# A block-sorted attention followed by a gated feed-forward layer: an earlier issue for the first weights, another place in the queue for batch 1's values, and rows of 72 elements for the mixed values

## The chip, the cores and the metric

The kernel runs on one core of one Trainium2 chip. The metric is the device time of one execution in microseconds (us); lower is better. Five engines work beside each other and meet through semaphores: PE (TensorE, matrix products; PEld in the profile is its loading of the stationary operand), DVE (VectorE), ACT (ScalarE), POOL (GpSimd) and SP (SyncE). Transfers between device memory and on-chip SBUF run on 16 DMA engines. PSUM holds the results of matrix products until DVE or ACT moves them to SBUF.

## The reference

```python
# B, H, S, D = 4, 8, 768, 64; 8 blocks of 96 rows; d_model 512, d_ff 1536
P = sort_net                                   # (B, H, 8, 8)
for _ in range(5):                             # Sinkhorn: rows, then columns
    P = exp(P - max(P, -1)); P = P / sum(P, -1); P = P / sum(P, -2)
k_sorted = einsum('bhij,bhjcd->bhicd', P, k_blocks)   # mix whole blocks
v_sorted = einsum('bhij,bhjcd->bhicd', P, v_blocks)
scores = q_blocks @ k_sorted.T / sqrt(D)       # inside a block: 96 x 96
attn = softmax(scores); o = attn @ v_sorted    # (B, H, S, D)
x = o as (B*S, H*D)                            # 3072 tokens of 512
g = x @ w_gate; out = (silu(g) * (x @ w_val)) @ w_out
```

## The kernel before

**Stages.** All loads are cast to bf16 on the way. The Sinkhorn iterations run first, on DVE and ACT, while batch 0's values, queries and keys arrive. The mixing weights P become a block matrix (`rmix`), and PE mixes the blocks of values (`v_chunk`, L275), keys (`k0_chunk`, L264, for batch 0; `kq_chunk`, L244, for the others) with it. Batch 0's attention for the first half of the tokens is written out by hand. From there on the feed-forward layer runs in eight steps `ffn(0)` to `ffn(7)`, one for each half batch of 384 tokens: 12 column blocks, each a gate product (`gate`, L385) and a value product (`value`, L403) of four matmuls, and with each step the output products of the step before (`outp`, L420). ACT takes the tanh of a gate product (L393), DVE makes gate times sigmoid of it (`gs_sb`, L395), and DVE multiplies the value product by that (`h`, L408).

**The order on PE.** PE and POOL run in the order in which the program writes them. `merge` places side work among the feed-forward products: a side item carries a due time, and it goes out once the running cost of the products written (0.65 for a gate or value product, 0.87 for a third of an output product) has reached it. These due times are numbers in the code, not measurements. In `ffn(1)` the side work is the mixing of batch 1: four `v_chunk` of 16 of the 64 value columns each, then three `kqs` items of two `kq_chunk` each, then the attention of batch 1 (`units`). DVE and ACT are ordered by a scheduler in that stage.

**PSUM.** Gate, value and early output products share three buffers (tag "gen"), so a product waits until DVE has read the product three before it. The mixes use two wide buffers, "a" and "b", in turn; each is drained by DVE or ACT (`drain`, L222 and L224).

**Loads.** POOL issues all loads, in one queue, and in between it copies values into a layout with the 96 rows of a block innermost (`copy_v`, L124, from `v_tiles` to `vch`); a `v_chunk` reads `vch` and needs all copies of its columns. Each POOL copy of 64 x 1536 elements is one quarter of the rows of a block. The order at the start: batch 0's values in two halves, the first query load, batch 0's keys in two halves, three copies, the first weights, the second query load, more weights with batch 1's values among them, batch 1's keys and queries, the output weights. The weights of `w_gate` and `w_val` come in six pairs of 256 columns each, which is two column blocks of the feed-forward layer:

```python
    def load_gv(lo, hi):
        load_w(wg_sb, wg_dram, lo, hi)
        load_w(wv_sb, wv_dram, lo, hi)
```

After these, POOL waits for batch 1's values, copies them (four copies), and issues the loads for batches 2 and 3.

**The mixed values.** `vt_tile` holds the mixed values, for each batch, head and block one row of 64 values, a one (its product gives the sum of the softmax), and padding. `av` (L334) multiplies the exponentials of a block (stationary, 96 x 128) by 65 elements of such a row; one call is eight matmuls over two heads and four blocks, in the order of the rows:

```python
                nc.tensor.matmul(o[:, two, i4, 0:D + 1], lhsT=e[:, i4 * C:i4 * C + 128],
                                 rhs=vt[:, 2 * g + two, half * 4 + i4, 0:D + 1],
```

There are 32 calls of `av`, four in the part written by hand and 28 among the feed-forward products.

Of the kernel before, what the change touches and what calls it, by code (L numbers as in the profile page):

```python
# [10 lines left out]
BF16 = mybir.dt.bfloat16  # L11
# [6 lines left out]
def kernel(  # L18
# [13 lines left out]
    B, H, S, D = q.shape  # L32
    NB = sort_net.shape[-1]
    C = S // NB
# [5 lines left out]
    DF = moe_w_gate.shape[1]  # L40
# [17 lines left out]
    vtp = ctx.enter_context(tc.tile_pool(name="vtp", bufs=2))  # L58
# [32 lines left out]
    def load_k(b, lo, hi):  # L91
        rows = highr if b else lowr
        nc.gpsimd.dma_start(out=kq_tile(b)[rows, lo:hi, :], in_=k_nat[b, :, lo:hi, :])
# [10 lines left out]
    def load_v(b, lo, hi):  # L104
        if b // 2 not in v_tiles:
            v_tiles[b // 2] = vnp.tile([128, C, D], BF16, name=f"v{b // 2}", tag="vn")
        u = b % 2
        nc.gpsimd.dma_start(out=v_tiles[b // 2][u * R:(u + 1) * R, lo:hi], in_=v_nat[b, :, lo:hi, :])

    def load_w(sb, dram, lo, hi):  # L110
        nc.gpsimd.dma_start(out=sb[:, :, lo:hi], in_=dram[:, :, lo:hi])
# [5 lines that stand above are left out]
    def copy_v(eng, pair, rows, s, n=4, d0=0, d1=D):  # L117
        cs = slice(s * (C // n), (s + 1) * (C // n))
        dst = vch3[rows, d0:d1, cs]
        src = v_tiles[pair][rows, cs, d0:d1]  # L120
        if eng is nc.scalar:
            eng.copy(dst, src.transpose([0, 2, 1]))  # L122
        else:
            eng.tensor_copy(dst, src.transpose([0, 2, 1]))  # L124
# [16 lines left out]
    def load_q0(t):  # L141
        nc.gpsimd.dma_start(out=q0[t].rearrange("p c d -> p (c d)"), in_=q_runs[0, t])
# [4 lines left out]
    load_q0(0)  # L147
    for a, rows in enumerate(halves):
        nc.gpsimd.dma_start(out=k0[rows], in_=k_nat[0, :, a * HC:(a + 1) * HC, :])
    copy_v(nc.gpsimd, 0, lowr, 0)  # L150
    copy_v(nc.gpsimd, 0, lowr, 3)
    copy_v(nc.gpsimd, 0, lowr, 5, 8, 40, D)
    load_gv(0, 256)
    load_q0(1)
    for m in range(256, 1024, 256):
        load_gv(m, m + 256)
    load_v(1, 0, C)
    for m in range(1024, DF, 256):
        load_gv(m, m + 256)
    load_k(1, 0, C)  # L160
    load_q(1, 0, C)
    nc.gpsimd.dma_start(out=wo_sb, in_=wo_dram)
# [6 lines left out]

    def vt_tile(pair):  # L170
        if pair not in vts:
            t = vtp.tile([C, 2, H * NB, D + 4], BF16, name=f"vt{pair}", tag="vt")
            nc.vector.memset(t[:, :, :, D:D + 1].rearrange("p u n e -> p (u n) e"), 1.0)
            vts[pair] = t
        return vts[pair]

    for pair in range(B // 2):
        vt_tile(pair)
# [59 lines left out]
    def kq_chunk(b, at, n, eng, tag):  # L238
        dst = kqt_tile(b)[:, 0:2 * GI * C].rearrange("p (n c) -> p n c", c=C)
        rm = rmix[b].rearrange("p a (g two) i -> p two (a g) i", two=2)  # L240
        tp = chunk_tile("tkq", n // 8, tag).rearrange("p (l n) -> p l n", n=2 * GI)
        for lc in range(n):
            for two in range(2):
                nc.tensor.matmul(tp[two * D:(two + 1) * D, lc, :],  # L244
                                 lhsT=kq_tiles[b][:, at + lc, :],
                                 rhs=rm[:, two], start=True, stop=True)
        drain(eng, dst[:, :, at:at + n], tp.transpose([0, 2, 1]))
# [20 lines left out]
    def v_chunk(b, at, n, eng, tag):  # L268
        rows = slice(0, 128) if b % 2 else lowr
        dst = vt_tile(b // 2)[:, b % 2]  # L270
        mix = rmix[b][rows, 0].rearrange("p a b -> p (a b)")
        tp = chunk_tile("tv", n // 8, tag).rearrange("p (l n) -> p l n", n=H * NB)
        for ld in range(n):
            col = (at + ld) * C
            nc.tensor.matmul(tp[:, ld, :], lhsT=vch[rows, col:col + 128], rhs=mix,  # L275
                             start=True, stop=True)
        drain(eng, dst[:, :, at:at + n], tp[0:C].transpose([0, 2, 1]))
# [103 lines left out]
    def gate(n, m):  # L381
        xt = xts[divmod(n, 2)]
        g_ps = psum.tile([128, TW], FP32, name="g_ps", tag="gen", bufs=3)
        for kc in range(NKC):
            nc.tensor.matmul(g_ps, lhsT=wg_sb[:, kc, ts(m, 128)], rhs=xt[:, kc, :],  # L385
                             start=(kc == 0), stop=(kc == NKC - 1))
        gate_out(n, m, g_ps)
# [11 lines left out]
    def value(n, m):  # L399
        xt = xts[divmod(n, 2)]  # L400
        v_ps = bank_tile("v_ps", "x" if (n, m) == (0, 1) else "gen")[:, 0:TW]
        for kc in range(NKC):
            nc.tensor.matmul(v_ps, lhsT=wv_sb[:, kc, ts(m, 128)], rhs=xt[:, kc, :],  # L403
                             start=(kc == 0), stop=(kc == NKC - 1))
        value_out(n, m, v_ps)
# [7 lines left out]
    def outp(n, t3, part):  # L413
        b, half = divmod(n, 2)
        h_w = h_tiles[n]
        if part == 0:
            o_tiles[n] = bank_tile("o_ps", "x" if 2 <= n < 2 * B - 1 or n == 2 * B - 1 and t3 == 1 else "gen")
        o_ps = o_tiles[n]
        for m in range(part * 4, part * 4 + 4):
            nc.tensor.matmul(o_ps, lhsT=h_w[:, m, ts(t3, 128)], rhs=wo_sb[:, m, :],  # L420
                             start=(m == 0), stop=(m == NFC - 1))
        if part < 2:
            return
        o_sb = opool.tile([128, DM], FP32, name="o_sb", tag="o_sb")
        nc.scalar.copy(o_sb, o_ps)  # L425
        base = b * S + half * TW + t3 * 128
        nc.sync.dma_start(out=out[ds(base, 128), :], in_=o_sb)
# [113 lines left out]
    def units(b, us, ats, lags=(3.1, 3.1)):  # L541
        us = list(us)
        todo = []
        for n, at in enumerate(ats):
            u, u2 = us[2 * n:2 * n + 2]
            lag = lags[n]
            held = []
            todo.append((at, lambda u=u, u2=u2, held=held: (qk(b, u, "b"), held.append(scores(b, u2, "a")))))
            todo.append((at + 1.3, lambda u2=u2, held=held: exps(b, u2, *held[0])))
            for w, tag, t in ((u, "b", 1.9), (u2, "a", 3.6)):  # L550
                if b == 0 or b == 1 and u < H2:
                    todo.append((at + t, lambda w=w, tag=tag: av(b, w, tag)))
                    todo.append((at + t + lag, lambda w=w: drain("v", *xtr(b, w))))
                else:
                    todo.append((at + t, lambda w=w, tag=tag: (av(b, w, tag), x_dma(b, w))))
        return todo

    def kqs(b, ats):
        return [(at, lambda n=n: (kq_chunk(b, n * 32, 16, "v", "b"), kq_chunk(b, n * 32 + 16, 16, "s", "a")))
                for n, at in enumerate(ats)]  # L560

    def vs(f, size, ats):
        return [(at, lambda m=m: f(1, m * size, size, "sv"[m % 2], "ba"[m % 2])) for m, at in enumerate(ats)]
# [5 lines left out]
    def merge(main, side):  # L569
        done, k = 0.0, 0  # L570
        side = sorted(side, key=lambda t: t[0])
        for c, f in main:
            f()
            done += c
            while k < len(side) and side[k][0] <= done:
                side[k][1]()
                k += 1
        while k < len(side):
            side[k][1]()
            k += 1  # L580

    def ffn(n):
        todo = []
        for m in range(NFC):
            if n > 0 or m > 1:
                todo.append((0.65, lambda m=m: gate(n, m)))
            if n > 0 or m > 0:
                todo.append((0.65, lambda m=m: value(n, m)))
            ends = (6, 9, 11) if n == 1 else (3, 7, 11)
            if n > 0 and m in ends:  # L590
                for part in range(3):
                    todo.append((0.87, lambda t3=ends.index(m), part=part: outp(n - 1, t3, part)))
        return todo
# [9 lines left out]
    def q0_rest():  # L603
# [1 line left out]
        q0_chunk(1, 16, 8, "v", "a")  # L605

    merge(ffn(0), [(0.0, q0_rest)] + units(0, range(4, 8), (2.0, 6.6)))
    merge(ffn(1), vs(v_chunk, 16, (3.2, 3.9, 4.7, 5.5)) + kqs(1, (6.2, 8.2, 10.3))
          + units(1, range(4), (11.3, 16.4), (3.1, 2.5)))
    for s in range(4):  # L610
        copy_v(nc.gpsimd, 1, both, s)
# [43 lines left out]
```

## Time and profile before

| | |
|---|---|
| time, median of 3 runs | 248.45 us (248.39 to 252.37) |
| profiled execution | 249.62 us |
| its span, first to last instruction | 247.7 us |
| TensorE clock granted | 1.000 |
| PE busy | 239.4 us, 97% |
| DVE, ACT, POOL busy | 157.1, 109.5, 51.9 us |
| loads through POOL's queue | 14.16 MB |

The profile is of one execution, and every time of a row is counted in us from the span's first instruction. The time of an execution contains the span and what lies around it, here 249.62 against 247.7. Matmuls overlap, so a busy time of PE that is close to the span says that PE hardly ever stops, not that each matmul is at its best. A row's idle time is that of its engine just before it; the name behind the arrow is the last event that was seen before the engine went on.

### The profile page before, as it was taken

How to read it: one execution, taken by the hardware profiler on the slowest of the kernel's cores; microseconds unless marked ns; L12 is line 12 of the kernel's file. 1: busy time of each engine (PE TensorE's matmuls, PEld its weight loads, DVE VectorE, ACT ScalarE, POOL GpSimd, SP SyncE). 2: the span in 40 equal slices, each digit the busy share in tenths (PEclk: the TensorE clock that was granted, in tenths of full speed). 3: DMA queues.
4: the chain of work that ended last, by engine and by line, in shares of the span. 5: the costliest groups of instructions: out<-in, count | busy, mean ns of one | idle time of the engine just before them, and what ended most of it. 6: DMA issues, size and time to landing. Idle time of an engine off the chain costs nothing.

```text
span 247.7 us, 6185 instructions
## 1 busy us (share of the span) xinstructions
PE 239.4 (97%) x2633; PEld 140.7 (57%) x2633; DVE 157.1 (63%) x332; ACT 109.5 (44%) x186; POOL 51.9 (21%) x45
## 2 busy tenths in 40 slices
PE   8799998999999999999999999999999999999995
PEld 6375665666555556655555655565555555555543
DVE  6686789787556775857657646755764585446700
ACT  3877652453544444444642552354245334232311
POOL 5993459960049300000000000000000000000000
PEclk9999999999999999999999999999999999999999
DMA  5999999999999287010122121112111121100122
GB/s 98 214 120 181 218 191 219 194 227 215 215 164 179 41 201 173 4 42 3 45 56 52 55 62 34 44 42 78 32 42 45 39 57 54 42 21 25 42 81 88
DMA packets 39578, 24.38 MB, mean 98 GB/s; under 512 B 27712, under 2 KB 35648, under 8 KB 39104
## 3 DMA queue, kind: packets, MB, share of 16 engines
q0 software_dynamic: 21376, 14.16, 39.3%
q1 hardware_dynamic: 18176, 9.84, 13.9%
q8 instruction: 20, 0.33, 0.5%
q14 instruction: 6, 0.05, 0.1%
HBM read 28.32 MB, written 7.86 MB: 146 GB/s over the span
## 4 chain that ended last, share of the span: by engine, by line
PE 83%; DVE 9%; ACT 2%; issue 2%; DMA 2%; DVEq 0%; POOLq 0%
PE v_ps L403 23%; PE o_ps L420 23%; PE g_ps L385 22%; PE tkq L244 3%; PE av_ps L334 2%; PE qk L307 2%; DVE st L340 2%; DMA v<-in_v_dram 2%; DVE gs_sb L395 2%; DVE h L408 2%; DVE vt L222 1%; PE o_ps L436 1%; PE idle_ps L446 1%; PE tv L275 1%; ACT th_sb L393 1%
## 5 line engine op out<-in xcount | busy, mean ns | idle before, releaser
L395 DVE SCALAR_TENSOR_TENSOR gs_sb<-th_sb,g_ps 128x384 bf16<-128x384 bf16 x96 | 52.8, 550 | 51.5 <-ACT th_sb L393 48.7
L403 PE MATMUL v_ps<-xt,wv_sb 128*128 128x384 bf16 x380 | 77.3, 326 | 1.1 <-DVE st L340 0.7
L385 PE MATMUL g_ps<-xt,wg_sb 128*128 128x384 bf16 x376 | 76.7, 326 | 0.1
L393 ACT ACTIVATE th_sb<-g_ps 128x384 bf16<-128x384 f32 x96 | 47.1, 490 | 57.0 <-PE g_ps L385 54.5
L420 PE MATMUL o_ps<-wo_sb,h 128*128 128x512 bf16 x276 | 64.0, 379 | 0.0
L408 DVE SCALAR_TENSOR_TENSOR h<-v_ps,gs_sb 128x384 bf16<-128x384 f32 x96 | 53.3, 555 | 6.9
L403 PEld LDWEIGHTS <-wv_sb 128*128 128x128 bf16 x380 | 35.1, 97 | 24.9 <-issue 1.9
L385 PEld LDWEIGHTS <-wg_sb 128*128 128x128 bf16 x376 | 34.7, 97 | 23.5 <-issue 0.4
L420 PEld LDWEIGHTS <-h 128*128 128x128 bf16 x276 | 26.3, 98 | 28.9
L425 ACT COPY o_sb<-o_ps 128x512 f32<-128x512 f32 x23 | 13.5, 585 | 50.9 <-PE o_ps L420 50.9
L124 POOL COPY vch<-v 64x1536 bf16<-64x1536 bf16 (+2 forms) x11 | 28.6, 2635 | 21.1 <-DMA v<-in_v_dram 21.0
L320 ACT ACTIVATE e_all<-qk 96x768 bf16<-96x768 f32 x30 | 22.6, 802 | 7.6 <-PE qk L307 7.6
L340 DVE TENSOR_TENSOR st<-av_ps,r_sb 96x512 bf16<-96x512 f32 x32 | 21.7, 679 | 0.2
L334 PEld LDWEIGHTS <-e_all 96*128 96x128 bf16 x256 | 12.0, 97 | 4.9 <-ACT e_all L320 0.9
L334 PE MATMUL av_ps<-vt,e_all 96*128 96x65 bf16 x256 | 13.2, 193 | 0.0
L222 DVE CAST vt<-tv 96x1024 bf16<-96x1024 f32 (+1 forms) x9 | 9.8, 1096 | 2.6 <-PE tv L285 1.6
L338 DVE RECIPROCAL r_sb<-av_ps 96x8 f32<-96x8 f32 x32 | 6.4, 199 | 8.0 <-PE av_ps L334 7.9
L224 ACT CAST vt<-tv 96x1024 bf16<-96x1024 f32 (+1 forms) x9 | 8.1, 913 | 3.0 <-PE tv L285 1.8
L446 PE MATMUL idle_ps<-warm_sb 128*128 128x512 bf16 x25 | 7.7, 416 | 0.0
L222 DVE COPY oh_sb<-o_ps 128x256 f32<-128x256 f32 x1 | 0.4, 423 | 9.3 <-PE o_ps L436 9.3
L122 ACT COPY vch<-v 64x768 bf16<-64x768 bf16 (+1 forms) x4 | 5.4, 1375 | 0.7 <-DMA v<-in_v_dram 0.7
L370 POOL DMA_DIRECT2D q_scr<-in_q_dram x2 | 5.7, 3228 | 0.0
(80 smaller groups left out, 135.3 us busy)
## 6 DMA issues: line engine op xcount, KB each, us to landing
out_dram<-o_sb SPq DMA_DIRECT2D x23, 256.0 KB, 2.0
v<-in_v_dram POOLq DMA_DIRECT2D x3, 768.0 KB, 19.9
wg_sb<-in_moe_w_gate_dram POOLq DMA_DIRECT2D x6, 256.0 KB, 11.1
wv_sb<-in_moe_w_val_dram POOLq DMA_DIRECT2D x6, 256.0 KB, 11.9
wo_sb<-in_moe_w_out_dram POOLq DMA_DIRECT2D x1, 1536.0 KB, 23.8
kp<-in_k_dram POOLq DMA_DIRECT2D x2, 768.0 KB, 15.1
q_scr<-in_q_dram POOLq DMA_DIRECT2D x2, 768.0 KB, 29.9
v<-in_v_dram POOLq DMA_DIRECT2D x2, 384.0 KB, 6.4
```

What stands on the lines that cost most here:

```text
L124: eng.tensor_copy(dst, src.transpose([0, 2, 1]))
L222: nc.vector.tensor_copy(dst, src)
L320: nc.scalar.activation(e_all[:, n:n + 2, 0:4 * C], wide[0:C, :, 0:4 * C], AF.Exp, scale=scale)
L334: nc.tensor.matmul(o[:, two, i4, 0:D + 1], lhsT=e[:, i4 * C:i4 * C + 128], rhs=vt[:, 2 * g + two, half * 4 + i4, 0:D + 1], start=True, sto ...
L340: nc.vector.tensor_tensor(st.rearrange("p i two d -> p two i d"), o[0:C, :, :, 0:D], r_sb.to_broadcast([C, 2, 4, D]), op=ALU.mult)
L385: nc.tensor.matmul(g_ps, lhsT=wg_sb[:, kc, ts(m, 128)], rhs=xt[:, kc, :], start=(kc == 0), stop=(kc == NKC - 1))
L393: nc.scalar.activation(th_sb, g_ps, AF.Tanh, scale=0.5)
L395: nc.vector.scalar_tensor_tensor(gs_sb, th_sb, 1.0, g_ps, op0=ALU.add, op1=ALU.mult)
L403: nc.tensor.matmul(v_ps, lhsT=wv_sb[:, kc, ts(m, 128)], rhs=xt[:, kc, :], start=(kc == 0), stop=(kc == NKC - 1))
L408: nc.vector.scalar_tensor_tensor(h_tiles[n][:, m, :], v_ps, 0.5, gs_tiles.pop(m), op0=ALU.mult, op1=ALU.mult)
L420: nc.tensor.matmul(o_ps, lhsT=h_w[:, m, ts(t3, 128)], rhs=wo_sb[:, m, :], start=(m == 0), stop=(m == NFC - 1))
L425: nc.scalar.copy(o_sb, o_ps)
```

## The change

Three things change.

1. On POOL, the first pair of weights (columns 0 to 255) is issued right behind batch 0's keys, ahead of the three copies; before, it was issued behind them.
2. On POOL, batch 1's values are issued behind the pair of columns 1024 to 1279 and ahead of the last pair; before, they were ahead of both. In `ffn(1)` the four `v_chunk` and the three `kqs` items get later due times. In the program built from it, the first `v_chunk` stands behind the gate product of column block 3 instead of block 2, and the first `kqs` item behind the value product of block 5 instead of block 4; the third `kqs` item and the attention of batch 1 stay in their places.
3. The rows of the mixed values are 72 bf16 elements apart instead of 68.

The same loads, copies, matmuls, activations and vector operations run as before.

```diff
     load_q0(0)
     for a, rows in enumerate(halves):
         nc.gpsimd.dma_start(out=k0[rows], in_=k_nat[0, :, a * HC:(a + 1) * HC, :])
+    load_gv(0, 256)
     copy_v(nc.gpsimd, 0, lowr, 0)
     copy_v(nc.gpsimd, 0, lowr, 3)
     copy_v(nc.gpsimd, 0, lowr, 5, 8, 40, D)
-    load_gv(0, 256)
     load_q0(1)
-    for m in range(256, 1024, 256):
+    for m in range(256, 1280, 256):
         load_gv(m, m + 256)
     load_v(1, 0, C)
-    for m in range(1024, DF, 256):
-        load_gv(m, m + 256)
+    load_gv(1280, DF)
     load_k(1, 0, C)
     load_q(1, 0, C)
     nc.gpsimd.dma_start(out=wo_sb, in_=wo_dram)
...
-            t = vtp.tile([C, 2, H * NB, D + 4], BF16, name=f"vt{pair}", tag="vt")
+            t = vtp.tile([C, 2, H * NB, D + 8], BF16, name=f"vt{pair}", tag="vt")
...
-    merge(ffn(1), vs(v_chunk, 16, (3.2, 3.9, 4.7, 5.5)) + kqs(1, (6.2, 8.2, 10.3))
+    merge(ffn(1), vs(v_chunk, 16, (4.5, 5.2, 5.9, 6.6)) + kqs(1, (7.3, 8.9, 10.5))
           + units(1, range(4), (11.3, 16.4), (3.1, 2.5)))
```

## The prediction

> **What bounds the kernel now.** I read the page's busy table first, then its DMA row, then the timeline around the one long stop of the matrix engine, then the timeline of POOL, which issues all loads.
>
> ```profile
> PE 239.4 (97%) x2633; PEld 140.7 (57%) x2633; DVE 157.1 (63%) x332; ACT 109.5 (44%) x186; POOL 51.9 (21%) x45
> DMA  5999999999999287010122121112111121100122
> ```
>
> PE is busy for 97% of the span. Only two things can shorten this kernel: a stop of PE that goes away, or a matmul that takes less time. The DMA engines are full from slice 2 to slice 13 (about 6 to 80 us), so in that stage a load lands when the queue gets to it, and its place in the queue counts. The stop is here:
>
> ```profile
> 40.32 0.81 PE L385 MATMUL g_ps<-xt,wg_sb 128*128 128x384 bf16 x4
> 40.83 0.56 DVE L408 SCALAR_TENSOR_TENSOR h<-v_ps,gs_sb 128x384 bf16<-128x384 f32 x1
> 40.97 0.34 PE L351 MATMUL x_ps<-ident,st 96*128 96x96 bf16 x4
> 41.90 0.54 DVE L395 SCALAR_TENSOR_TENSOR gs_sb<-th_sb,g_ps 128x384 bf16<-128x384 bf16 x1
> 41.99 0.44 PEld L403 LDWEIGHTS <-wv_sb 128*128 128x128 bf16 x4 [0.84 <-DMA wv_sb<-in_moe_w_val_dram]
> 42.00 0.82 PE L403 MATMUL v_ps<-xt,wv_sb 128*128 128x384 bf16 x4 [0.70 <-DVE st L340]
> 42.66 0.81 PE L385 MATMUL g_ps<-xt,wg_sb 128*128 128x384 bf16 x4
> ```
>
> Columns: start, length, engine, line, and in brackets the idle time before it with what ended it. The four transposes at 40.97 leave PE free at 41.14. The next value product stands still until 42.00, because its weight load waits for the last value weights (columns 1280 to 1535), which land at 41.95 in the trace. The matmul's own bracket names DVE's st, but that is only the last event before it: by the program, this product's PSUM buffer is released by the gate product of column block 9, whose DVE operation starts at 40.19 and takes 0.54. So DMA alone holds PE, for 0.86.
>
> The queue itself has a hole, early on (columns: window, its length, busy time with instruction counts by engine, clock, DMA share, GB/s):
>
> ```profile
> 12.00:13.00 1.00, 1.00 (x50) 0.93 (x47) 0.44 (x2) 0.24 (x2) 1.00 (x3) 1.00 0.67 135
> 13.00:14.00 1.00, 0.93 (x32) 0.84 (x29) 0.72 (x2) 1.00 (x2) 1.00 (x2) 1.00 0.09 18
> 14.00:15.00 1.00, 0.99 (x32) 0.97 (x31) 1.00 (x1) 0.52 (x2) 1.00 (x3) 1.00 0.54 47
> ```
>
> The DMA share falls to 0.09 because POOL copies values and issues nothing:
>
> ```profile
> 3.53 1.07 POOL L149 DMA_DIRECT2D qk<-in_k_dram  x2
> 6.57 6.34 POOL L124 COPY vch<-v 64x1536 bf16<-64x1536 bf16 x3 [1.97 <-DMA v<-in_v_dram]
> 12.85 0.79 POOL L111 DMA_DIRECT2D wg_sb<-in_moe_w_gate_dram  x1
> 34.99 11.17 POOL L124 COPY vch<-v 64x1536 bf16<-64x1536 bf16 x4 [1.56 <-DMA v<-in_v_dram]
> ```
>
> **Part 1, the first weights ahead of the copies.** The two issues move from 12.85 to 4.60, where POOL idles 1.97. They took 0.79 and 0.77, so they end at 6.16, before the values land at 6.51, and the copies start at 6.57 as now. If an issue takes longer, there is more cover: the first mix of the values runs at 12.82, right after the query products, and the copy that it needs from POOL ends near 12.2, so 0.35 + 0.6, about 1 us, is free. Beyond that each us of issue costs one at the head. Behind the moved issues stand the three copies and the second query load, whose issue comes 1.5 earlier. The keys stay ahead in the queue (last half landed at 14.49, first read at 15.03).
>
> The gain is that all later loads move up. The queue loses 0.33 + 0.91 + 0.46 = 1.7 in the three windows. But a load counts as landed with its last of 16 engines, and that one lags: the keys end on it at 14.49, the first weights at 16.94, and weights later take 1.33 each there (25.28, 26.61, 27.95), so its hole is 16.94 - 14.49 - 1.33 = 1.1. Bounds 0 and 1.7; I take 1.1, since the last engine gives the release.
>
> The Trainium skill speaks against this move: "SBUF — State Buffer", in the part on SBUF's two separate sides, says that POOL cannot write descriptors while DVE holds the shared port, and gives some 3.1 us instead of 0.62 for a load issued next to a DVE copy. As an estimate by that page, two such issues would end near 10.8 and push the head back by about 3. The row next to it is the keys' pair above: 1.07 for two issues, with DVE in the same small fp32 work. I go by the row.
>
> **Part 2, batch 1's values behind one more weight pair.** The three loads values, gate weights, value weights (landed 34.87, 36.18, 37.56) become gate, value, values: the values land when the third did, 37.56 - 1.1 = 36.46. The weights of columns 1024 to 1279 come earlier and were not waited for. The last pair has the same bytes ahead as before and lands at 41.95 - 1.1 = 40.85, so the stop at 42.00 goes. Each later issue of POOL waits for the landing eight loads back and keeps ahead of the queue (the values' issue waits for about 23.1, their turn comes near 33).
>
> What is late next? The value product starts at 41.14, the gate product at 41.79 (its buffer is free at 41.39), the last value product at 42.50 (it waits for the DVE row at 41.90, which ends at 42.44), the transposes at 43.15. The copy of their result to SBUF, behind DVE's gate work, held batch 0's second half until 44.91; now gate work ends at 43.70, the copy at 44.02, PE goes on at 44.08. **Gain 0.83**; bounds 0 (queue not moved) and 0.86.
>
> POOL's four copies of batch 1's values take 11.17 from 36.46 + 0.12, to 47.75. The four mixes of these values move one gate and one value product down: the first stood at 47.70 and stands at 47.70 - 0.83 + 2 x 0.65 = 48.17. Slack 0.4 (1.5 before). Behind the copies POOL issues the loads for batches 2 and 3, at 47.75 instead of 46.11; the queue is then still on the output weights (landed 56.16), so no hole.
>
> **Part 3, the new spacing.** From gate block 2 of batch 0's second half to the first output product PE took 58.24 - 47.06 = 11.18, of which 10 products of 0.65, 4 mixes of 0.47, 2 key/query mixes of 1.13 and their two exits of 0.12 make 10.88. So 0.3 are stops, the largest 0.23 where the second half of the first key mix waits for DVE's drain of the last value mix. Laid out in the new order with DVE's 1.21 per drain and 0.54 per gate or value step, the same wait stays at about 0.19 and the others go. **Gain 0.1**, bounds -0.3 (a second drain of 1.21 half uncovered) and 0.3.
>
> **Part 4, rows of 72 elements.**
>
> ```profile
> L334 PE MATMUL av_ps<-vt,e_all 96*128 96x65 bf16 x256 | 13.2, 193 | 0.0
> 31.03 0.41 PE L334 MATMUL av_ps<-vt,e_all 96*128 96x65 bf16 x8
> 31.29 0.81 PE L403 MATMUL v_ps<-xt,wv_sb 128*128 128x384 bf16 x4
> 47.70 0.63 PE L275 MATMUL tv<-rmix,vch 128*128 128x64 bf16 x16
> 48.17 0.81 PE L403 MATMUL v_ps<-xt,wv_sb 128*128 128x384 bf16 x4
> ```
>
> Eight attention products take 0.26 (32 ns each), sixteen mixes of nearly the same width 0.47 (29 ns each). The single start times in the trace show why: within the eight, the steps are 34.5, 32.9, 29.2, 32.6, 29.1, 33.2, 29.2 ns (means of 32 sets). Every odd one costs 33. Its row of 68 bf16 starts at an odd multiple of 136 bytes, 8 past a multiple of 16; the even ones start on one. The stationary operand steps by 192 bytes in both kinds of product, and the mixes do not alternate, so it is the row. With 144 bytes all rows start alike: 4 x 4 = 16 ns for each of the 32 sets. The head's four and the four before the wait on DVE at 44.08 are mostly covered, so 24 x 0.016, **gain 0.38**; bounds 0 and 32 x 8 x 0.004 = 1.0. The drains that write these rows stay: they take 1215 ns (DVE) into 136-byte rows and 1219 into the 192-byte rows of the keys.
>
> The skill has a rule here ("SBUF — State Buffer", Door 1, the note on cachelines): lines of 16 bytes, and each crossing costs. A row of 130 bytes touches nine lines from either start, so by that count nothing is gained and the sum would be 0.93. The row shows 4 ns, and it decides.
>
> **Sum.** 0.83 + 0.1 + 0.38 = 1.3. The profiled execution took 249.62 with a span of 247.7; both would fall by 1.3, to 248.3 and 246.4. That execution is 1.17 above the median of the runs, 248.45; from the median I get 247.1.
>
> **Rivals.**
> - *The rows give nothing.* For it: 4 ns is near the trace's grain. Against: 32 sets agree. 248.45 - 0.83 - 0.1 = 247.5.
> - *The queue does not move up*, because the lagging engine has other work in the hole. For it: landings hang on that one engine, up to 2 behind the others. Then the stop stays, the copies end at 48.85 against mixes at 49.0, and 0.48 is left: 248.0.
> - *Slower: PE waits for batch 1's values.* They are now the last of three loads, and POOL needs 11.3 after their landing. PE is at the first mix at 48.17, so any landing after 36.9 is paid one for one, and after 38.2 the gains of 1.3 are gone. For it: slack falls from 1.5 to 0.4. Against: before, the third load landed at 37.56 even with the hole. If the lag of 2 that the slow engine shows at worst falls on this load, it lands at 38.5 to 39: 248.45 - 1.3 + 1.9 = 249.0.
>
> **How the numbers follow.** Chances: forecast 0.55, rows alone 0.15, queue 0.15, slower 0.15. Range 246.3 (248.45 less the three upper bounds, 0.86 + 0.3 + 1.0) to 248.9, which leaves out the far end of the slower case. Two per cent, 5 us, is about what a measurement of this kernel can tell from no change; no case here comes near, so within 2% has 0.96, each side 0.02.
>
> **What would show it.** Right: no DMA bracket before the value product near 41; the DMA share near 1 at 13 to 14; POOL's first copies still at 6.57, the later four from about 36.6; the first mix with no wait for POOL; all steps of the attention products at 29 ns. Wrong: first copies later than 7.5, a weight load on vch that waits for POOL, or a new DVE wait between 47 and 62.

## The result and the profile after

| | before | after |
|---|---|---|
| median, first comparison (6 runs each) | 248.49 us (248.37 to 252.37) | 249.93 us (249.54 to 250.59) |
| ratio after / before | | 1.006, interval 1.0044 to 1.0075 |
| profiled execution, span | 249.62, 247.7 us | 249.54, 247.7 us |

The changed kernel is 0.6% slower, with the whole interval above 1. The forecast was 247.1, faster by 1.3. The two profiled spans are equal, and that is the first thing to explain: the fastest run of after is 249.54, but 248.37 of before, so the trace of before that the prediction read was a slow sample of a faster kernel.

The page of after (one line was taken out of the source, so its line numbers are one or two lower than those of before):

```profile
PE 236.6 (96%) x2609; PEld 140.5 (57%) x2633; DVE 157.1 (63%) x332; ACT 109.8 (44%) x186; POOL 52.0 (21%) x45
...
DMA  5999999999996187010122121112111111100122
...
q8 instruction: 20, 0.33, 0.5%
```

PE is still the bound. Its busy time fell, which is no gain: 24 matmuls have no record in this trace, and PE has new stops. The DMA row is full one slice less. The third line stands word for word in the page of before too, where I passed over it: a queue of 20 packets with 0.33 MB in all, 16 KB each, of the kind "instruction".

Most of the signs that the prediction named came out as forecast. The hole in the queue is gone (windows; before: 0.09 in the first of these):

```profile
13.00:14.00 1.00, 0.92 (x32) 0.83 (x29) 0.98 (x2) 1.00 (x2) 1.00 (x3) 1.00 1.39 190
14.00:15.00 1.00, 0.86 (x31) 0.84 (x28) 1.00 (x2) 0.53 (x2) 1.00 (x2) 1.00 1.45 196
...
17.00:18.00 1.00, 0.25 (x17) 0.25 (x18) 0.53 (x1) 0.44 (x1) 1.00 (x2) 1.00 1.22 191
```

POOL's copies start on time (timeline of POOL; 6.57 and 34.99 before), and the value product behind the transposes no longer waits for its weights (timeline; 40.97 and 42.00 before):

```profile
4.57 0.83 POOL L111 DMA_DIRECT2D wg_sb<-in_moe_w_gate_dram  x1
5.34 0.80 POOL L111 DMA_DIRECT2D wv_sb<-in_moe_w_val_dram  x1
6.27 6.40 POOL L124 COPY vch<-v 64x1536 bf16<-64x1536 bf16 x3
...
33.75 11.20 POOL L124 COPY vch<-v 64x1536 bf16<-64x1536 bf16 x4 [5.49 <-DMA v<-in_v_dram]
```

```profile
41.50 0.34 PE L350 MATMUL x_ps<-ident,st 96*128 96x96 bf16 x4
...
41.67 0.81 PE L402 MATMUL v_ps<-xt,wv_sb 128*128 128x384 bf16 x4
```

But the transposes themselves are late: 41.50 instead of 40.97. The window from 17 to 18 above shows where that comes from: PE is busy for 0.25 of it, against 0.91 before. The timeline of after has two stops that before has not, both in the middle of a product, with every operand on chip. Before, the key mix runs through in one row:

```profile
15.25 1.92 PE L264 MATMUL tk<-rmix,qk 128*64 128x64 bf16 x96
```

After, it breaks off behind 91 of its 96 matmuls:

```profile
14.98 1.83 PE L263 MATMUL tk<-rmix,qk 128*64 128x64 bf16 x91
...
17.75 0.26 PE L263 MATMUL tk<-rmix,qk 128*64 128x64 bf16 x5 [0.94 <-issue]
...
61.01 0.44 PE L243 MATMUL tkq<-rmix,kq 128*64 128x64 bf16 x16 [0.46 <-issue]
```

"issue" in the bracket means that the profile shows no event that PE waited for. The first stop is in the last key mix of batch 0, the second in a key mix of batch 1. Neither place was touched by the change.

**What PE waits for.** PE has 5268 instructions in this program, and 20 packets of 16,384 bytes on the instruction queue make one for every 256 of them, 64 bytes each. Counted in the order of the built program, the first stop stands at number 695 and the second at number 1975, which is exactly 5 x 256 behind it. (The expectations below call the first place 719; they mean the same instruction.) The trace has this packet (window 15.3 to 16.3 of the DMA view of after; columns: packets, MB, share of 16 engines):

```profile
q0 software_dynamic: 169, 0.21, 119.6%
q8 instruction: 1, 0.02, 5.6%
```

The record of this packet starts at 15.38 and takes 0.89, and PE goes on at 17.75, which is 1.48 behind its end. The reading is that PE had run out of instructions. The next section tests it.

### The profile page after: what moved, and what is told of

Same layout as the page of the kernel before. It is cut to its first block, busy times and chain, and to the rows that moved or that the text cites. A ratio compares the mean times of both kernels' runs of the same rounds, so it can differ in the third digit from the quotient of the medians.

```text
span 247.7 us, 6162 instructions
## 1 busy us (share of the span) xinstructions
PE 236.6 (96%) x2609; PEld 140.5 (57%) x2633; DVE 157.1 (63%) x332; ACT 109.8 (44%) x186; POOL 52.0 (21%) x45
## 4 chain that ended last, share of the span: by engine, by line
PE 83%; DVE 8%; issue 3%; ACT 2%; DMA 2%; DVEq 0%; POOLq 0%
PE v_ps L402 23%; PE g_ps L384 23%; PE o_ps L419 22%; PE tkq L243 3%; PE av_ps L333 3%; PE qk L306 2%; DMA v<-in_v_dram 2%; DVE st L339 2%; DVE gs_sb L394 2%; DVE h L407 1%; DVE vt L221 1%; PE o_ps L435 1%; PE idle_ps L445 1%; PE tv L274 1%; PE tk L263 1%
## 5 line engine op out<-in xcount | busy, mean ns | idle before, releaser
L419 PE MATMUL o_ps<-wo_sb,h 128*128 128x512 bf16 x255 | 61.5, 379 | 1.3 <-issue 0.2
L445 PE MATMUL idle_ps<-warm_sb 128*128 128x512 bf16 x22 | 6.1, 381 | 0.3 <-issue 0.3
```

## The experiments

Two explanations stood against each other. **A:** the hole in the load queue, which the prediction counted as waste, is where the refill of PE (the packets with its next instructions) got through; the earlier weights fill it. **C:** the loss lies in the new spacing of `ffn(1)` or in the rows of 72. A third point, **B**, is about the sample: the stop at 42 in the first trace of before is not there in most executions.

### The kernel before, once more

No edit.

> The unchanged kernel once more, for a second trace and spans of its timed runs. Theory A (PE's refills of instructions are held up by the full queue of loads): the trace has the stop of about 0.8 us before the value product at 42, no stop without a named releaser at 17 to 18, span 247 to 248. Theory B (the first trace of the kernel before was not typical, the stop at 42 is mostly absent): no DMA bracket at 42, or one under 0.3 us, and a span near 246.6; time 248.5 either way.

Measured: 248.63 (248.43 to 251.57, 10 runs), span 246.6. B holds: there is no stop at 42. The stop that the expectation under A put there is missing; of A's signs only the absence of a stop at 17 to 18 came out. The timeline of this execution at the place of the stop:

```profile
40.78 0.34 PE L351 MATMUL x_ps<-ident,st 96*128 96x96 bf16 x4
...
40.95 0.81 PE L403 MATMUL v_ps<-xt,wv_sb 128*128 128x384 bf16 x4
```

The value product follows the transposes at once. The last value weights landed at 39.81, not at 41.95. The 0.83 that the prediction took from this stop is not there to be had in a typical run.

### Each part alone

Part 1 alone:

```diff
+    load_gv(0, 256)
     copy_v(nc.gpsimd, 0, lowr, 0)
     copy_v(nc.gpsimd, 0, lowr, 3)
     copy_v(nc.gpsimd, 0, lowr, 5, 8, 40, D)
-    load_gv(0, 256)
```

> Only the first weights are issued ahead of the three copies. Theory A: PE stands for about 0.9 us near 17.7 in the middle of the key mixes with no releaser named, the refill packet starts near 15.4 instead of 14.2; the stop at 42 is gone; time from 248.5 to 250. Theory C (the loss is in the new spacing or in the rows of 72): no slower than before, 247.6 to 248.5.

Part 2 alone (batch 1's values behind the pair of columns 1024 to 1279, and the later due times):

```diff
-    for m in range(256, 1024, 256):
+    for m in range(256, 1280, 256):
         load_gv(m, m + 256)
     load_v(1, 0, C)
-    for m in range(1024, DF, 256):
-        load_gv(m, m + 256)
+    load_gv(1280, DF)
...
-    merge(ffn(1), vs(v_chunk, 16, (3.2, 3.9, 4.7, 5.5)) + kqs(1, (6.2, 8.2, 10.3))
+    merge(ffn(1), vs(v_chunk, 16, (4.5, 5.2, 5.9, 6.6)) + kqs(1, (7.3, 8.9, 10.5))
```

> Only batch 1's values behind one more weight pair, with the later due times. Theory A: no stop near 17.7, the stop at 42 stays, time 248.2 to 248.6. Theory C: the loss of about 1.4 us is here, 249.5 to 250.

Part 3 alone (`D + 8` for `D + 4` in `vt_tile`):

> Only the rows of 72 elements. Theory A: the attention products' steps of 33 ns fall to 29, time 248.0 to 248.4. Theory C: slower than 248.8.

Measured, against 248.74 for before (31 runs on the same chip):

| | median (lowest to highest) | ratio (interval) | span |
|---|---|---|---|
| part 1 alone | 249.58 (249.31 to 250.15) | 1.0027 (1.0006 to 1.0047) | 247.7 |
| part 2 alone | 249.60 (248.68 to 250.70) | 1.0033 (1.0009 to 1.0057) | 247.8 |
| part 3 alone | 248.39 (248.32 to 250.22) | 0.9995 (0.9974 to 1.0015) | 246.4 |

Part 1 alone makes the whole of the stop, at the same instruction and the same time (timeline of part 1 alone):

```profile
17.75 0.26 PE L264 MATMUL tk<-rmix,qk 128*64 128x64 bf16 x5 [1.05 <-issue]
```

This is A against C: neither the spacing nor the rows are in this kernel. Part 1 also does what it was forecast to do: all its ten runs lie within 0.84, while before scatters over 2.6, and no stop stands at 42. As far as these runs tell, it takes away the late landings and puts 1 us in their place in every run.

For part 2 alone the expectation was missed: it was to cost nothing, and costs 0.9. Its profiled execution has no stop in the head, but the stop at the value product (timeline of part 2 alone):

```profile
41.78 0.44 PEld L402 LDWEIGHTS <-wv_sb 128*128 128x128 bf16 x4 [0.82 <-DMA wv_sb<-in_moe_w_val_dram]
41.78 0.82 PE L402 MATMUL v_ps<-xt,wv_sb 128*128 128x384 bf16 x4 [0.68 <-DVE st L339]
```

As in the first trace of before, the last pair landed late, here at 41.74. The runs of part 2 alone spread from 248.68, near the quick runs of before, to 250.70, which would fit late landings that come more often rather than a constant cost. Only one execution was profiled, so this is not shown, nor is why the order of values and weights should do it.

### Parts 2 and 3 without part 1

> Late values with the new spacing and rows of 72, the first weights where they were. Theory A: no stop near 17.7; the stop at 42 in a part of the executions, as for late values alone; 248.4 to 249.6. Theory C: 249.6 to 250.

Measured: 249.33 (248.53 to 251.07), ratio 1.0028 (1.0005 to 1.005), no stop in the head. The profiled execution shows another wait (timeline):

```profile
48.51 0.64 PE L274 MATMUL tv<-rmix,vch 128*128 128x64 bf16 x16 [0.39 <-POOL vch L124]
```

This is the slower rival of the prediction, PE waiting for POOL's copies of batch 1's values. The values landed at 37.14; the prediction had set 36.9 as the point from which a landing is paid one for one. In after itself they land at 33.62, and the row has no wait. So this mechanism is real, and part 1 is all that differs between the two kernels (one trace of each).

### Another load in the hole

The weights stay where they were, and the load of batch 1's keys goes into the hole instead:

```diff
+    load_k(1, 0, C)
     copy_v(nc.gpsimd, 0, lowr, 0)
...
-    load_k(1, 0, C)
     load_q(1, 0, C)
```

> The kernel before with batch 1's keys, a load that nobody needs before 40 us, issued behind batch 0's keys instead of the first weights. Theory A: any load in the hole holds up the refill: packet start 15 or later, an unnamed stop of 0.5 to 1.5 us at PE instruction 719 in the last key mix, near 17.7. If the weights themselves are the cause (their 512-byte pieces, their landing), no stop there.

Measured: 250.50 in one run, span 248.4, clock 1.0. The stop is at the same instruction, and twice as long (timeline):

```profile
18.73 0.26 PE L264 MATMUL tk<-rmix,qk 128*64 128x64 bf16 x5 [1.90 <-issue]
```

So it is not the weights as such, nor their early issue. Another load that fills the hole is enough, and this larger one (0.75 MB against 0.5 MB) costs more in its one run.

### Moving the instruction count under the work

Fewer idle matmuls at the start shift every later PE instruction to a lower number, so that the boundary of 256 falls on later work. `dots(124)` issues 124 matmuls with their weight loads (two instructions each) in the first 5 us. With 12 fewer in the kernel after:

> The changed kernel with 12 idle matmuls left out, 24 PE instructions. Theory A: the stop of about 0.9 us is there, but 24 instructions later in the program, in the query mix after the key mixes instead of in the last key mix. Any cause that hangs on data (keys, buffers) leaves it at the same key mix, or removes it.

With 25 fewer in the kernel after, and, as the control, in before:

> The changed kernel with 25 of the 124 idle 32x32 matmuls at the very start left out, so every later PE instruction stands 50 places earlier (two per matmul). Theory A (refills): the block that PE lacks begins 50 instructions further on in the program, at the first score products, where PE waits for ACT anyway; no stop near 17.7, none of 0.46 near 61 in the last key mix; 1 us or more gained, 248.0 to 248.6. Theory C (spacing, rows) or a delay of the keys: still 249.6 to 250.

> The kernel before with the same 25 idle matmuls left out: the control. Theory A: its refills were in time, so nothing changes, 248.3 to 248.8. If leaving them out gains by itself, it gains here too, below 248.0.

With 72 more in the kernel after, and, as the control, in before:

> The changed kernel with 72 more idle 32x32 matmuls at the start (about 1.9 us in which PE waits for the Sinkhorn steps anyway), 144 PE instructions. Theory A (refills): the block that PE lacked at instruction 719 is asked for while PE still stands at the Sinkhorn steps, before 11 us, so its packet starts before 11 and PE has no unnamed stop between 11 and 23, though the queue of loads is as full as in the changed kernel; 248.0 to 248.5. If the loss hangs on the keys, the copies or the weights themselves: unchanged, 249.5 to 250.

> The kernel before with the same 72 idle matmuls: the control. Theory A: 248.3 to 248.8, as before, with executions up to 2 longer where the last value weights land late. If the idle matmuls gain or cost by themselves, it shows here.

Measured:

| | median (lowest to highest) | ratio to before (interval) | granted clock |
|---|---|---|---|
| after, 12 fewer | 251.59, one run | | 1.0 |
| after, 25 fewer | 251.75 (250.25 to 252.71) | 1.009 (1.0031 to 1.0149) | 0.993 in 3 of 6 |
| before, 25 fewer | 249.13 (248.45 to 250.86) | 0.9998 (0.9967 to 1.003) | 1.0 |
| after, 72 more | 252.67 (250.59 to 253.76) | 1.0115 (1.0042 to 1.0189) | 0.993 in 3 of 4 |
| before, 72 more | 253.2 (252.74 to 253.49) | 1.0148 (1.008 to 1.0215) | 0.992 or 0.993 in all |

The place follows A exactly. With 12 fewer the stop leaves the key mix and stands 24 instructions later in the program, in the query mix; with 25 fewer it stands 50 later, at the first scores (timelines of the two kernels):

```profile
19.33 0.32 PE L253 MATMUL tq<-sel,qk 128*64 128x64 bf16 x9 [1.77 <-issue]
```

```profile
20.84 0.34 PE L306 MATMUL qk<-kqt 64*128 64x96 bf16 x8 [2.42 <-issue]
```

In both, it is number 695 of PE's instructions. In each of the four traces that have the stop and every matmul record (part 1 alone, after with 12 and with 25 fewer, before with 25 fewer) 350 matmuls stand ahead of it. With 72 more, the stop falls earlier into the key mixes, and a further one comes at number 951, 256 behind. No operand, tile or engine explains a stop that stays with the number while the work under it changes.

The times went another way than expected. Moving the boundary was meant to remove the stop or leave it; in each case the packet also came later or the stop came on worse work. With 72 more in after the packet was to start before 11; PE asked for it at 12.02, it started at 14.34, and a stop of 0.92 was there. And 72 more idle matmuls cost as much in before as in after, so this lever is no clean one: it moves every boundary. With 72 more, before has its stop at number 951 (21.97, 1.93 long), and then something else falls (windows, before with 72 more; the column behind POOL's is the granted clock):

```profile
20.00:22.00 2.00, 0.07 (x3) 0.03 (x2) 0.00 (x0) 1.11 (x3) 0.00 (x0) 1.00 1.26 170
22.00:24.00 2.00, 2.00 (x34) 1.42 (x34) 1.66 (x5) 0.55 (x2) 1.51 (x2) 0.88 1.43 193
24.00:26.00 2.00, 1.78 (x21) 1.47 (x20) 1.30 (x5) 1.30 (x3) 0.84 (x3) 0.50 1.48 204
26.00:28.00 2.00, 2.00 (x13) 1.04 (x12) 0.78 (x2) 0.30 (x1) 1.19 (x2) 0.77 1.46 196
```

From 1.5 us behind the stop on, the granted clock is halved for about 3.4 us (0.12, 0.50 and 0.23 of full speed are missing in the last three windows, of 2 us each). The same happens with 25 fewer in after (0.51 from 22 to 24, 0.63 from 24 to 26, behind the stop that ends at 20.84), and the six runs of that kernel fall into two groups by it: 250.25 to 250.93 at clock 1.0, 252.58 to 252.71 at 0.993. The Trainium skill, "TensorE: Matmul & The Clock Gate", in its part on the clock gate, has TensorE fall back to half its clock behind an idle window of some 3.4 us. The halving is in this trace, but the idle time ahead of it was 1.93 us, shorter than the figure of the page. After with 72 more has the half clock too (0.57 from 16 to 20), with a stop of only 0.92 in it, so the stop alone does not set it; what does is open.

### Half of part 1

If the refill needs room, a smaller load should leave it. This kernel is before with rows of 72, and with only the gate half of the first pair ahead of the copies:

```diff
+    load_w(wg_sb, wg_dram, 0, 256)
     copy_v(nc.gpsimd, 0, lowr, 0)
     copy_v(nc.gpsimd, 0, lowr, 3)
     copy_v(nc.gpsimd, 0, lowr, 5, 8, 40, D)
-    load_gv(0, 256)
+    load_w(wv_sb, wv_dram, 0, 256)
```

> The kernel before with rows of 72 elements, and with only the gate half of the first weight pair ahead of the three copies; the value half stays behind them, and batch 1's values keep their place. The hole in the load queue becomes about 1.35 us shorter instead of vanishing, and later loads land some 0.5 to 1 us earlier.
> A (the 16 KB refill of PE's instructions has to find room in the load queue): a hole is left, from about 14.0 to 14.9, so the refill packet that lies around 14.2 in the kernel before starts at 14.0 to 14.7, PE resumes at most at 16.1, and no stop stands at PE's instruction 719; the last value weights land before 41.5, so the stop near 42 is rare, and with the 0.2 of the rows the median is 248.2 to 248.5.
> C (it is the earlier issue of the weights as such that costs, not the refill): half of the loss of 1 us appears, 248.8 to 249.2.
> If the refill packet starts after 15.3, the stop is back in the last key mix, with about 1 us, and the time is that of the kernel after, 249.3 to 249.9; then even one load too many takes the room.

Measured: 248.33 (248.25 to 248.51, 12 runs) against 248.54 (248.35 to 250.21, 17 runs) for before, ratio 0.9978 (0.9962 to 0.9994), span 246.5. By the ratio to before this is the fastest version of the study, and its runs scatter by 0.26, while 5 of the 17 runs of before lie above 249. The packet starts at 13.97, and PE passes number 695 without a stop (windows, DMA view from 13.9 to 14.9, and timeline of this kernel from 16 on, where its row begins in the middle of the key mixes):

```profile
13.00:14.00 1.00, 0.92 (x33) 0.83 (x30) 0.99 (x2) 1.00 (x2) 1.00 (x3) 1.00 1.43 205
```

```profile
q0 software_dynamic: 330, 0.16, 131.9%
q8 instruction: 1, 0.02, 5.6%
```

```profile
15.81 1.05 PE L265 MATMUL tk<-rmix,qk 128*64 128x64 bf16 x55
```

The last value weights land at 36.93, and nothing stops near 42. So the earlier landings that part 1 was to bring can be had without its cost; the median gains 0.2 by them and the rows together. One detail of the expectation was wrong: no hole is left that a window shows, since the share is 1.43 where the refill goes through, as high as the 1.39 of after. One thing that differs is how long the second weight load had stood in the queue when PE asked near 13.3: its issue ran from 12.40 to 13.16 here, and had ended at 6.14 in after. Which property of the queue lets the packet through, the share of all 16 engines does not show.

### The refill in all kernels

From the packet records and the order of PE's instructions (us; "asked" is where PE reaches number 439, one block before the one that runs out, which I take for the request since no record shows it):

| | asked | packet starts | PE at 695 | stop |
|---|---|---|---|---|
| part 2 alone | 13.45 | 13.71 | 16.73 | none |
| rows of 72 alone | 13.35 | 13.72 | 16.63 | none |
| parts 2 and 3 | 13.48 | 13.89 | 16.76 | none |
| before, once more | 13.45 | 13.90 | 16.73 | none |
| before, first trace | 13.63 | 14.23 | 16.91 | none |
| half of part 1 | 13.32 | 13.97 | 16.60 | none |
| before, 72 more | 11.72 | 12.89 | 15.42 | none |
| before, 25 fewer | 14.25 | 16.17 | 18.75 | 0.42 |
| after | 13.36 | 15.38 | 17.75 | 0.94 |
| part 1 alone | 13.25 | 15.35 | 17.75 | 1.05 |
| after, 72 more | 12.02 | 14.34 | 16.82 | 0.92 |
| after, 12 fewer | 14.23 | 16.98 | 19.33 | 1.77 |
| keys in the hole | 13.39 | 16.25 | 18.74 | 1.90 |
| after, 25 fewer | 14.35 | 18.53 | 20.84 | 2.42 |

That this is the request fits the number of packets: 20 with 5268 instructions, 21 with 144 more. In the kernels that leave at least half of the first pair behind the copies, the packet comes 0.3 to 0.65 later, 1.2 in one case; where the whole pair or batch 1's keys stand ahead of the copies, 2.0 to 4.2. Before with 25 fewer is between them with 1.9: it asks when its hole closes (the first weights are issued from 12.86 on). How busy the engines are in sum does not tell the groups apart, since half of part 1 has its packet in time at a share of 1.43. The packet takes 0.9 to 1.1, and PE goes on 1.4 to 1.6 behind its end. At the rate of this stage PE has about 3.2 us between asking and running out, so a delay above some 0.8 is a stop. Where PE is slower through its instructions, a delay costs nothing: in the first trace of before the next packet is asked for at 16.88 and starts at 22.07, and PE, which needs it at 26.34, does not stop.

The Trainium skill, "DMA: Bandwidth & Descriptors", in the part on queues, rings and completion order, says that each DMA engine takes turns between its queue rows at the grain of one packet, of 9 to 17 descriptors as a rule and 64 at most. In after, the 742 load records from 13.4 to 15.3 make one per 41 ns on each of 16 engines, so as an estimate by that page a turn would be waited for 0.4 to 0.7 us, 2.6 at most. The measured 1.9 to 4.2 lie above the first figure and partly above the second, so one turn of such a packet does not explain all of it. In after and in part 1 alone the packet starts to the hundredth when the first gate weights have landed (15.38 and 15.35), as if it stood behind that whole load; in the kernel with the keys in the hole it does not coincide with a landing. What exactly the packet waits for stays open.

## Why the prediction was wrong, point by point

- **What bounds the kernel.** Right, but incomplete. PE was rightly held to gain only by fewer stops or shorter matmuls, but I counted as possible new stops only waits for operands and buffers. That PE needs instructions, which come as DMA packets among the loads, was in none of the terms and in none of the rivals.
- **Part 1, its cost at the head, set at nothing: the step that failed.** What it said of POOL came out: issues of 0.83 and 0.80 (forecast 0.79 and 0.77), no 3.1 us as the rule weighed there would have it, copies at 6.27. The 1 us of cover was examined for POOL and DVE only. The real price is the stop of 0.94 at 17.75; against the second trace of before, the first gate product is 0.74 later (23.91 against 23.17). The hole of 1.7, or 1.1 on the last engine, was counted as lost time: PE's refill came through in it.
- **The queue moves up by 1.1.** Right in kind, and too small: the first pair landed 1.6 earlier than in the first trace of before, the last value weights at 36.46, which is 3.35 earlier than in its second trace (39.81).
- **Gain 0.83 from the stop at 42.** Wrong for the median. The stop was in one execution, which was 1.17 above the median, and most of that distance was this stop. I noted the distance and still took the 0.83 from the median as well. In the second trace of before it is absent, and the right term there is about 0. What part 1 does remove, as far as its ten runs tell, is the tail of before's runs.
- **The slower rival** (PE waits for batch 1's values) had the right sign and the wrong place for after: no such wait is in it. The mechanism showed, with 0.39, only where part 1 was left out.
- **The new spacing, 0.1.** From the first gate product to the first output product after wins 0.15 on the second trace of before (0.74 late, then 0.59), of which the rows make 0.01 (rows alone takes 34.00 for this stretch, before 34.01). So 0.1 is left for the order, as forecast, from one trace of each; no wait of PE for an operand shows in this stretch.
- **Rows of 72, 0.38.** Right in part, and the size off. Rows alone end 0.20 earlier (last matmul 243.04 against 243.24), but half of that is there at the first key mix (14.96 against 15.07), ahead of any attention product; the rows make 0.1. The steps inside a set of eight are now 34.4, 29.7, 29.2, 29.8, 30.1, 33.0, 29.7: of the four long ones two went and two stayed, so a set gains 4.8 ns and not 16, and 32 sets would make 0.15. The median shows no difference from 1 (0.9995, 0.9974 to 1.0015). That the first step stays at 34.4 shows that it never came from the row.
- **A second stop, in no term:** 0.46 at 61.01, at number 1975, and 0.16 behind it. There the request fell at 55.25, later than in the second trace of before (54.65), and its packet started at 58.59 instead of 56.35. At batch 1's first scores after is 1.25 late, where it was 0.59 late at the first output product.

In sum, against the second trace of before: +0.74 from the stop in the head, -0.15 up to the first output product, +0.66 around the second stop, -0.11 from there to the last matmul, 1.14 in all (244.38 against 243.24; the spans 247.7 and 246.6). The median of after lies 0.4 above its profiled execution; no trace of those runs shows why, and part 2, which alone raises the median, is a possible reason that was not tested.

Three readings of the first trace would have shown the risk: the line of the instruction queue, the time of its second packet (14.23, inside the hole), and PE at number 695 at 16.91, 0.25 behind what that packet allows (14.23 + 0.96 + 1.47 = 16.66, with the 1.4 to 1.6 that the stops show between a packet's end and PE). With so little to spare a delay of 1 us shows.

## What to carry to other kernels

A hole in a transfer queue is not free room until you know who else uses the DMA engines in it: look for the instruction queue in the list of queues, divide the engine's instructions by its packets, and see which work stands a block behind each packet. A stop named "issue" in the middle of a product, which stays at the same instruction number when the work under it moves, is the engine out of instructions; take something out of the queue around the request, or make the load there smaller, rather than look at operands. And subtract a stop from the median only if a second profile of the same kernel shows it.

## What the runs showed of the hardware that was not expected

- PE's instructions come in packets of 16,384 bytes, one for 256 instructions (20 in this program). PE resumed 1.3 to 1.6 us behind the end of a late packet, and a late packet cost 0.4 to 2.4 us.
- Loads of 0.5 MB in the hole (as the list of transfers has their size) delayed the packet by 2.0 to 2.3 us (2.8 and 4.2 where fewer idle matmuls moved the count), one of 0.75 MB by 2.9; one of 0.25 MB left it in time (0.65, against 0.45 and 0.6 in the two traces of before).
- A stop of about 2 us was followed, in some executions, by about 3.4 us at half the granted clock, 1 to 1.5 us later. That lengthened the run by about 2 us more (after with 25 fewer: 250.25 to 250.93 and 252.58 to 252.71).
- With rows of 144 bytes in place of 136, two of seven steps between products of 65 columns fell from 32.9 and 32.6 to 29.7 and 29.8 ns; two others stayed at 34.4 and 33.0.
